# First product of three pairs of token groups by one level of Strassen

## The chip, the core and the metric

The kernel runs on one core of a Trainium2 chip. The core has a matrix engine (TensorE, in the profile PE, its weight loads PEld), a vector engine (VectorE, DVE), a scalar engine (ScalarE, ACT), GpSimd (POOL) and SyncE (SP), which here only issues DMAs; sixteen DMA engines move data between DRAM and the on-chip memory. Matmuls write to PSUM, which has eight banks of 128 x 512 float32. Every engine works through its own queue in order and waits on semaphores for the others. The metric is the device time of one execution in microseconds (us).

## What is computed

For each of 8 batches the reference makes a linear attention with 8 heads, 576 positions and 64 dimensions per head: softmax of k over the positions, softmax of q over the dimensions, `kv = k_s^T v`, and `x = q_s kv`. The 8 x 576 = 4608 rows of x, 512 wide, then go through a gated network:

```python
h = x @ w_in          # 512 -> 2048
g = h * np.cos(h)
out = g @ w_out       # 2048 -> 512
```

All of it is in float32. A float32 value is used by TensorE in two ways here: as one slower float32 matmul, or as the sum of a high and a low part in the rounded type float32r, with three matmuls (high x high, high x low, low x high).

## The kernel before

**Groups and units.** The 4608 tokens are nine groups of 512: 512 tokens of each batch (groups 0 to 7), and the 64 tokens left of each of the eight batches together (group 8, kept in DRAM in `x_left` until then). The 2048 columns of w_in are 16 blocks f of 128. A *unit* is one group with one f. `unit1` makes its first product, h = x w_in[f] (4 chunks of the 512 inputs x 3 matmuls = 12 matmuls into one PSUM bank, L866), and the gate: `turns` on ACT (L872), `rest` on DVE (L876), `cos` on ACT (L882), `gate` on DVE (L888), then the split into `ghi` on ACT (L892) and `glo` on DVE (L896). `unit2` makes the second product, g w_out[f], 4 x 3 matmuls (L935) that accumulate over f in four PSUM banks `acc`; it stands two units behind `unit1`. The first six units use float32 matmuls in the second product (L928). Groups 0 and 1 are interleaved by halves of the 16 f, with the half-finished output in DRAM (`part`); the others run over all f. `out_rows` takes the result from `acc` (ACT, L974, or with a part to be added DVE, L971) and writes it out.

**Weights.** The two weight matrices come as float64, are loaded raw (`load_w`), turned to float32 by two ACT and two DVE steps (`convert`) and split into high and low parts, which then stay on chip for all groups, w_in and w_out of each f beside each other (`w_io`) for f from 8 on.

**Attention.** `attend` for batch b is spread over the units of the group before it: `k_exps` (maximum over positions with GpSimd's all-reduce, L524, subtraction, exp), `k_steps` (kv, L571, and its normalisation), `q_steps` (softmax of q), `x_steps` (q transposed, from batch 2 on through DRAM in blocks; x product, `x_mm`, L730; x split by ACT `x_hi`, L744, and DVE `x_lo`, L758). For batches 0 and 1 (XF=2) `x_mm` is one float32 matmul; for the others it is three float32r ones, with kv and q split by L586, L606, L610 and L708, L718. Two PSUM banks, `att`, serve it; two, `h`, the first product.

**Order.** Nothing is issued in the order of the loops. Each step is put into a `Plan` with its engine, an estimated duration, the places that it reads and writes and, for some, a due time. `Plan.order` simulates all engines with these durations and latencies (the table `LAT`; ACT's table loads count only where `tables` is not zero, and it is 0) and picks each engine's next piece by priority among the ready ones; the order found is each engine's program order. Buffers are reused in rings (`BUFS`, `ring`).

All DMAs are issued by SP.

Of the kernel before, what the change touches and what calls it, by code (L numbers as in the profile page):

```python
# [27 lines left out]
    XF=2,  # L28
    PELO=1,
    early=1,  # L30
    F2=6,
# [12 lines left out]
    att1=(5.98, 6.97),  # L44
    att=dict(k=(0.32, 0.1), kv=(3.88, 1.0), q=(5.03, -0.91), qt=(22.82, 6.17), x=(4.44, 4.38)),
# [14 lines left out]
class Plan:  # L60
# [7 lines left out]
    LAT = {("ACT", "PE"): 0.37, ("DVE", "PE"): 0.3, ("DVE", "ACT"): 0.14, ("DVE", "DVE"): 0.13,  # L68
# [32 lines left out]

    def lat(self, i, j):

        a, b = self.steps[i], self.steps[j]
        return self.LAT.get((a[0], b[0]), 1.0 if a[0] == "BUS" else 0.2)

    def run(self, edges, prio, release=None, tables=False):
# [14 lines left out]
        for _ in range(n):  # L122
# [12 lines left out]
            while w and w[0][0] <= t:  # L135
                at, i = heappop(w)
                heappush(c, (at if e == "BUS" else prio[i], i))
# [57 lines left out]
def linear_attention_then_cos_gated_mlp(  # L195
# [54 lines left out]
    mask = const.tile([P, 2, 1], F32, name="mask")  # L250
    nc.vector.memset(mask, 0.0)
    nc.vector.memset(mask[0:D, 0], 1.0)
    nc.vector.memset(mask[D:P, 1], 1.0)
# [12 lines left out]
    def v_frame(t):  # L266
# [15 lines left out]
    part = dr.tile([2, NJ, P, DM], F32, name="part")  # L282

# [5 lines left out]
        x4k=8, kq=2, qm=1, qs=2, ql=1, mt=1, m1=1, m=2, r=2, kvt=1, kvw=4, xl=4, stage=2, wc=1, r2=3, ghi=2,  # L289
        glo=2, h=2, acc=4, att=2, qb=1, qf=1, qd=2,  # L290
# [13 lines left out]
    def sbt(shape, dt, tag, name, bufs=None):  # L304
        pool = small if tag in SMALL else sb
        return pool.tile(shape, dt, tag=tag, name=name, bufs=bufs or BUFS[tag])


    for tag, size in (
        ("pad", NL), ("ql", NL), ("qm", 18), ("qs", 18), ("r", 1),  # L310
        *((f"w{w}{f}", 2 * DM) for f in range(CFG["FN"]) for w in "io"),
        *((f"w{f}", 4 * DM) for f in range(CFG["FN"], NF)),
        ("x4k", 2 * TB), ("r2", TB), ("ghi", TB), ("glo", TB), ("stage", TB), ("wc", 2 * DM),
        ("kvw", 2 * P), ("mt", 4 * P), ("m1", 2 * P), ("m", 2 * P), ("kvt", P), ("xl", NL), ("kq", 4 * NC * D), ("qt0", S), ("qt1", S), ("qb", S), ("qf", S),
    ):
        for i in range(BUFS.get(tag, 1)):
            sbt([P, size], F32, tag, f"place_{tag}_{i}", BUFS.get(tag, 1))

    def bank(tag, name):
        return ps.tile([P, 512], F32, tag=tag, name=name, bufs=BUFS[tag])  # L320
# [10 lines left out]
    def room(f):  # L331


        return ("room", NF - 1 - f // 4, f % 4)

    def rooms(f):
        return [("room", f, i) for i in range(4)]

    def spot(ws, f):
        return f"w{f}" if f >= FN else f"w{ws}{f}"  # L340

    def load_w(w, f, after=0.0, seq=()):
        def load():
            if ("raw", w, f) not in T:
                ws = w if f < FN else "io"
                a = sbt([P, len(ws), DM, 2], U32, spot(ws, f), f"raw_{ws}{f}", 1)
                for i, x in enumerate(ws):
                    T["raw", x, f] = a, a[:, i]
# [12 lines left out]
            1.5, load, writes=[("w", w, f)] + rooms(f), after=after if not seq else 0.0, seq=seq  # L361
        )

    def convert(ws, f):

        n = len(ws)
        R = [("w", w, f) for w in ws]
        wait = ws == "o" and f < F2
        C = room(f) if wait else ring("wc")

        def low():
            return T["raw", ws[0], f][0][:, :, :, 0]

        def high():
            return T["raw", ws[0], f][0][:, :, :, 1]
# [17 lines left out]
        def sign():  # L393
            if wait:
                if ("room", f // 4) not in T:
                    T["room", f // 4] = sbt([P, 4, DM], F32, f"w{NF - 1 - f // 4}", f"room_{f // 4}", 1)
                c = T["wc", ws, f] = T["room", f // 4][:, f % 4 : f % 4 + 1]
            else:
                c = T["wc", ws, f] = sbt([P, 2, DM], F32, "wc", f"wc_{ws}{f}")[:, 0:n]
# [739 lines left out]
```

## Time and profile before

| | |
|---|---|
| Median of 3 runs | 889.59 us (889.19 to 890.18) |
| Span of the profiled execution | 885.9 us |
| Mean granted TensorE clock | 0.992 |
| Matmuls | 4336 |

The profile is of one execution; for it the page gives the span, from the first to the last instruction, and no time of its own. What lies around the span is taken from the median, 3.7 us. In the rows of groups, the columns are line, engine, operation, output and inputs with partitions and elements, the count, busy time in us and mean ns of one, and the idle time of the engine just before them with what ended it. In rows of the timeline they are start and length in us, engine, line, operation. In rows by stretch they are the stretch, its length, the busy time of PE, PEld, DVE, ACT and POOL with counts, the granted clock, the busy share of the DMA engines and GB/s. DMA rows give the size in KB and the us from issue to landing.

### The profile page before, as it was taken

Reading aid. Unit: us, or ns where it says so; the run is one execution under the profiler, and the core shown is the slowest. Engines: PE = TensorE matmul, PEld = TensorE weight load, DVE = VectorE, ACT = ScalarE, POOL = GpSimd, SP = SyncE. Lnnn points to the kernel's source line nnn. Section 1 sums busy time; section 2 is a strip of 40 time slices with the busy share of each in tenths; the row PEclk is TensorE's granted clock in tenths of the full one; section 3 lists DMA queues with packets and bytes.
Section 4 is the critical chain, followed back from the end, with each engine's and each line's share of the span. In section 5 each row is a group of like instructions: output and inputs, shape, how many; then the busy total and the mean of one; then the engine's idle time right before and its main releaser. Section 6 shows DMA issues by size and latency. Waiting matters only on the chain.

```text
span 885.9 us, 11763 instructions
## 1 busy us (share of the span) xinstructions
PE 866.2 (98%) x4336; PEld 705.2 (80%) x4336; DVE 555.0 (63%) x924; ACT 487.7 (55%) x812; POOL 30.3 (3%) x61
## 2 busy tenths in 40 slices
PE   6989999999999999999999999999999999999997
PEld 5656788887888888888888888888888888888885
DVE  7888888977686457745775568646853353333332
ACT  3898798566445545653675456635633353333332
POOL 1200100000000000100000000000000000000000
PEclk8999999999999999999999999999999999999999
DMA  8971656532363026302540046103410020001002
GB/s 228 293 214 35 203 182 185 142 106 76 84 177 82 1 57 180 84 2 57 134 117 15 22 122 140 41 4 105 109 25 1 3 96 1 1 0 48 1 1 48
DMA packets 167225, 75.75 MB, mean 86 GB/s; under 512 B 111360, under 2 KB 157952, under 8 KB 167168
## 3 DMA queue, kind: packets, MB, share of 16 engines
q1 hardware_dynamic: 167168, 75.00, 31.4%
q8 instruction: 34, 0.56, 0.3%
q14 instruction: 23, 0.19, 0.1%
HBM read 55.31 MB, written 19.66 MB: 85 GB/s over the span
## 4 chain that ended last, share of the span: by engine, by line
PE 90%; ACT 4%; DMA 2%; SPq 2%; DVE 1%; issue 1%; ACTq 0%
PE acc L935 42%; PE h L866 42%; PE x_False L730 3%; PE kv L571 2%; PE acc L928 1%; DMA k<-in_k_dram 1%; DMA raw_o<-in_moe_w_out_dram 1%; SPq L467 1%; ACT raw_o L378 0%; DMA v_sb<-in_v_dram 0%; SPq L463 0%; ACT w_i L409 0%; ACT L882 0%; ACT L646 0%; ACT raw_i L383 0%
## 5 line engine op out<-in xcount | busy, mean ns | idle before, releaser
L866 PE MATMUL h<-x,w_i 128*128 128x512 f32 x768 | 186.4, 391 | 0.5 <-DVE g L888 0.3
L866 PE MATMUL h<-x,w_io 128*128 128x512 f32 x768 | 185.4, 390 | 0.9 <-DVE kt L888 0.9
L935 PE MATMUL acc<-w_io,ghi 128*128 128x512 f32 x576 | 178.2, 390 | 0.1
L876 DVE SCALAR_TENSOR_TENSOR kt<-kt,h 128x512 f32<-128x512 int32 x144 | 98.4, 683 | 124.6 <-ACT kt L872 124.1
L872 ACT ACTIVATE kt<-h 128x512 int32<-128x512 f32 x144 | 86.0, 597 | 159.3 <-PE h L866 158.9
L866 PEld LDWEIGHTS h<-x,w_i 128*128 128x128 f32 x768 | 143.3, 188 | 31.2 <-ACT x L756 0.6
L866 PEld LDWEIGHTS h<-x,w_io 128*128 128x128 f32 x768 | 143.1, 188 | 30.9 <-DVE kt L888 1.5
L935 PE MATMUL acc<-w_o,ghi 128*128 128x512 f32 x528 | 163.8, 391 | 0.0
L888 DVE TENSOR_TENSOR kt<-kt,h 128x512 f32<-128x512 f32 x138 | 94.6, 685 | 76.1 <-ACT kt L882 75.2
L882 ACT ACTIVATE kt<-kt 128x512 f32<-128x512 f32 x144 | 91.1, 633 | 84.3 <-DVE kt L876 83.9
L892 ACT CAST ghi<-kt 128x512 fp32r<-128x512 f32 x138 | 85.5, 620 | 89.1 <-DVE kt L888 70.6
L896 DVE TENSOR_TENSOR glo<-kt,ghi 128x512 fp32r<-128x512 f32 x138 | 95.2, 690 | 62.7 <-ACT ghi L892 62.0
L935 PEld LDWEIGHTS acc<-w_io,ghi 128*128 128x128 f32 x576 | 107.2, 188 | 22.5 <-ACT o L974 0.8
L935 PEld LDWEIGHTS acc<-w_o,ghi 128*128 128x128 f32 x528 | 98.4, 188 | 20.5
L935 PE MATMUL acc<-w_io,glo 128*128 128x512 f32 x288 | 112.1, 389 | 0.0
L935 PE MATMUL acc<-w_o,glo 128*128 128x512 f32 x264 | 102.8, 389 | 0.0
L935 PEld LDWEIGHTS acc<-w_io,glo 128*128 128x128 f32 x288 | 54.1, 188 | 11.3
L935 PEld LDWEIGHTS acc<-w_o,glo 128*128 128x128 f32 x264 | 49.6, 188 | 10.4
L730 PE MATMUL x_False<-qt,kvw 128*128 128x288 f32 x176 | 34.9, 323 | 0.4 <-ACT qt L713 0.4
L744 ACT CAST x<-x_False 128x288 fp32r<-128x288 f32 x64 | 23.7, 370 | 18.2 <-PE x_False L730 18.2
L882 ACT ACT_TABLE_LOAD x26 | 33.4, 1283 | 0.4
L730 PEld LDWEIGHTS x_False<-qt,kvw 128*128 128x128 f32 x176 | 28.4, 191 | 5.5 <-POOL m L524 0.8
(103 smaller groups left out, 738.5 us busy)
## 6 DMA issues: line engine op xcount, KB each, us to landing
q<-in_q_dram SPq DMA_DIRECT2D x32, 256.0 KB, 3.4
out_dram<-o SPq DMA_DIRECT2D x32, 256.0 KB, 2.8
v_sb<-in_v_dram SPq DMA_DIRECT2D x30, 256.0 KB, 3.7
k<-in_k_dram SPq DMA_DIRECT2D x14, 512.0 KB, 4.6
qb<-q_rows SPq DMA_DIRECT2D x96, 72.0 KB, 2.5
q_rows<-q SPq DMA_DIRECT2D x24, 256.0 KB, 2.4
raw_i<-in_moe_w_in_dram SPq DMA_DIRECT2D x8, 512.0 KB, 5.5
raw_o<-in_moe_w_out_dram SPq DMA_DIRECT2D x8, 512.0 KB, 6.6
```

Source lines behind the costliest of these rows:

```text
L467: nc.sync.dma_start(t[NL * i : NL * (i + 1), 2 * CM, :].rearrange("p (h d) -> p h d", h=2), s2[:, NM:S, :].rearrange("h p d -> p h d"),)
L571: nc.tensor.matmul(x[h * D : (h + 1) * D, odd : odd + vt.shape[1]], t[:, h, c, :], vt, start=(c == CM), stop=(c == CM - 1),)
L730: nc.tensor.matmul(t[:, 0:HALF], a, c[:, cs], start=(n == 0), stop=(n == len(parts) - 1 and not again))
L744: nc.scalar.copy(T["x", b, p][:, 0, cs], o[:, 0 : cs.stop - cs.start])
L866: nc.tensor.matmul(o, a, x, start=(c == 0 and n == 0), stop=(c == KC - 1 and n == 2))
L872: nc.scalar.activation(t, T["h", u], AF.Identity, bias=0.25, scale=1.0 / TWO_PI)
L876: nc.vector.scalar_tensor_tensor(t.bitcast(F32), t, -TWO_PI, T["h", u], op0=ALU.mult, op1=ALU.add)
L882: nc.scalar.activation(t, t, AF.Sin, bias=0.5 * math.pi)
L888: nc.vector.tensor_mul(o, t, T["h", u])
L892: nc.scalar.copy(t, T["kt", u].bitcast(F32))
L896: nc.vector.tensor_sub(t, T["kt", u].bitcast(F32), T["gh", u].bitcast(F32))
L935: nc.tensor.matmul(T["acc", j], a[:, js], w, start=(first and n == 0), stop=(last and n == 2))
```

## The change

Groups 0 to 2 keep the form above (`std=3`). Groups 3 to 8 are worked in the pairs (3, 4), (5, 6), (7, 8). Within a pair, the first product of two groups and two blocks f, f+1 of w_in is made by one level of Strassen's scheme in Winograd's form: the 2 x 2 parts are the two groups by the two halves of the 512 inputs, and the two halves of the inputs by the two f. Seven products of sums of operands stand for eight, and further sums, made from the results in PSUM, give the four h.

- *Sums of w_in.* Each converted block of w_in is written to DRAM (`w_rows`, `keep`). During group 2 `sums(n)`, one for each of the 8 pairs of f, reads two of them, makes four sums on DVE, splits them and writes them, with the three operands that need no sum, to `w_sums` in DRAM. w_in itself then no longer stays on chip. In the pairs each `block` loads its seven operands (high and low parts) in four DMAs of up to 512 KB from POOL's queue, which converts float32 to float32r, into a ring of five buffers (`sr`, places of w_in 0 to 4).
- *Sums of x.* From batch 3 on x goes to DRAM whole (`x_main`, `x_row`). `x_sums` loads the two groups' halves and makes the seven operands on DVE and ACT, in places of w_in 8 to 15 and of x.
- *Products.* `block` issues seven products of 2 chunks x 3 matmuls, in turn into a bank of `h` and the second bank of `att`, which leaves one bank for the attention of later batches; three partial results are copied out by ACT and three added up by DVE, and the gates follow.
- *Second product.* Unchanged in form. `acc` has room for one group, so in each half of the 16 f (four blocks) the second products of one group (`now`) run among the blocks, and those of the other (`later`), whose g are kept in `stash`, after them. One group's output is parted by halves, as groups 0 and 1 were.
- *Attention.* `XF=8`: the x product is one float32 matmul for all batches, and the split of kv and q (`kv_norm`, `kv_hi`, `kv_lo`, `q_hi`, `q_lo`) is gone. Batches 3 and 4 are attended before the first pair, 5 and 6 beside it, 7 beside the second.
- *Places.* From f = 8 on, blocks of w_in, and of w_out, are converted in twos of the same matrix; buffers are named one by one.

The core of the diff:

```diff
-    XF=2,
+    XF=8,
...
+    std=3,
+    spans={2: (15.0, 28.0), 3: (24.0, 38.0), 4: (32.0, 47.0)},
...
+    def cast_load(self, us, fn, reads=(), writes=(), due=None):
+
+        t = object()
+        self.add("POOL", 1.1, fn, reads=reads, writes=[*writes, t], due=due)
+        self.add("SWB", us, None, reads=[*reads, t], writes=writes)
...
+        def keep():
+            for i, x in enumerate(fs):
+                nc.sync.dma_start(w_rows[x], T["wc", w, f][:, i])
...
+        if not keep:
+            for i in range(2):
+                plan.add("ACT", 0.4, lambda i=i: x_row(i), reads=[xo[i]], writes=[xs])
+            plan.load(0.9, put, reads=[xs], writes=[("x_main", p, b), ("x_left", p, b)], parts=2)
+            return []
...
+    def sums(n):
...
+        def adds():
+            t = T["sum", n].rearrange("p f (k d) -> p (f k) d", k=2)
+            a11, a12, a21, a22 = (t[:, i] for i in range(4))
+            nc.vector.tensor_add(a22, a21, a22)
+            nc.vector.tensor_sub(a21, a11, a21)
+            nc.vector.tensor_sub(a11, a22, a11)
+            nc.vector.tensor_sub(a12, a12, a11)
...
+    def x_sums(k, b1, b2):
...
+            for i, m, sub in (
+                (0, A0, None),
+                (1, A0, (A0, A1, A0)),
+                (2, A0, (A0, B1, A0)),
+                (3, B1, None),
+                (4, A1, (A1, B1, A1)),
+                (5, B0, None),
+                (6, B0, (B0, B0, A0)),
+            ):
+                if sub:
+                    plan.add(
+                        "DVE", 0.69, lambda sub=sub, move=move: move(*sub),
+                        reads=at(sub[1]) + at(sub[2]) + [st[0], st[1]], writes=at(sub[0]),
+                    )
+                xp = x_places(i, c)
+                plan.add("ACT", 0.62, lambda i=i, m=m, hi=hi: hi(i, m), reads=at(m) + [st[m[0]]], writes=xp)
+                plan.add("DVE", 0.69, lambda i=i, m=m, lo=lo: lo(i, m), reads=at(m) + [st[m[0]]], writes=xp)
...
+    def block(k, n, b1, b2, flip, due):
+
+        z, aux = ring("h"), ("att", 1)
+        c1, c5, c2 = (ring("c") for _ in range(3))
...
+        for m in range(4):
+            place = wide(ring("sr")[1])
...
+                nc.gpsimd.dma_start(t, w_sums[n, :, 2 * m : e])
+
+            plan.cast_load(
+                2.0 if m < 3 else 1.2, load, reads=[("sums", n, i) for i in range(3)],
+                writes=[place, (place, 0), (place, 1)],
+            )
+            ws.append(place)
...
+        def product(i, to, first):
+            if first:
+                T["z" + to, k, n] = bank(z if to == "z" else aux, f"{to}_{k}_{n}_{i}")
+            o = T["z" + to, k, n]
+            for c in range(2):
+                xh, xl = (T["xs", k, i, c][:, m] for m in range(2))
+                wh, wl = (T["s", k, n, i][:, m, c * P : (c + 1) * P] for m in range(2))
+                for m, (a, x) in enumerate(((wh, xh), (wh, xl), (wl, xh))):
+                    nc.tensor.matmul(
+                        o, a, x, start=(first and c == 0 and m == 0), stop=(c == 1 and m == 2),
+                        skip_group_check=not first,
+                    )
...
+        pe(0, "z", True)
+        copy("z", c1)
+        pe(1, "a", True)
+        copy("a", c5)
+        pe(2, "z")
+        copy("z", c2)
+        pe(3, "a")
+        add("a", c2)
+        G[b2, f] = post(0, b2, f, c2)
+        pe(4, "z")
+        add("z", c5)
+        G[b2, f + 1] = post(1, b2, f + 1, c5)
+        pe(5, "a", True)
+        add("a", c1)
+        G[b1, f] = post(2, b1, f, c1)
+        pe(6, "z")
+        G[b1, f + 1] = post(3, b1, f + 1, z)
+        return G
...
+    def pair(k, b1, b2, clk):
...
+        for half in range(2):
+            now, later = (b1, b2) if half == 0 else (b2, b1)
...
+            for n in range(NB * half, NB * half + NB):
+                G.update(block(k, n, b1, b2, half == 1, clk))
+                clk += 7 * 1.37 * phi
+                for e in range(2):
+                    if n > NB * half:
+                        f = 2 * (n - 1) + e
+                        second(now, n - 1, e, (now, f, f == 0, False, False, half == 0))
+                    split(now, n, e)
...
+            for n, e in fs:
+                f = 2 * n + e
+                if half == 0:
+                    what = (later, f, f == 0, False, False, False)
+                else:
+                    what = (later, f, f == NF // 2, f == NF - 1, True, False)
+                second(later, n, e, what)
...
+            if u == 2 * NF:
+                for n in range(NF // 2):
+                    sums(n)
+    for b in range(STD, min(STD + 2, B)):
+        attend(b, spans[b], ("att", "att", "att"))
+    clk = when(NU)
+    for pk, (b1, b2) in enumerate(PAIRS):
+        length = 29.3
+        at = (clk - T0) / U
+        for i, b in enumerate((b1 + 2, b2 + 2)):
+            if b < B:
+                attend(b, (at + 13 * i, at + 13 * i + 14), ("att", "att", "att"))
+        clk = pair(pk, b1, b2, clk)
```

More of the change, by code (lines that the diff above doesn't have):

```diff
@@ L288, in linear_attention_then_cos_gated_mlp @@
     BUFS = dict(
-        x4k=8, kq=2, qm=1, qs=2, ql=1, mt=1, m1=1, m=2, r=2, kvt=1, kvw=4, xl=4, stage=2, wc=1, r2=3, ghi=2,
-        glo=2, h=2, acc=4, att=2, qb=1, qf=1, qd=2,
+        x4k=8, kq=2, qm=1, qs=2, ql=1, mt=1, m1=1, m=2, r=2, kvw=4, xs=1, stage=2, wc=2, r2=3, ghi=2,
+        glo=2, h=2, acc=4, att=2, qb=1, qf=2, qd=2, sr=5, c=4,
     )
@@ L331, in room, with rooms, base, spot @@
     def room(f):
[L334 to L340, printed above, removed]
+        return ("room", NF - 2 - 2 * (f // 4), f % 4)
+    def rooms(w, f):
+        return [("room", f - f % 2, i) for i in range(4)] if w == "o" else []
+    def base(f):
+        return f if f < FN else f - f % 2
+    def spot(w, f):
+        return f"w{w}{base(f)}"
     def load_w(w, f, after=0.0, seq=()):
@@ L360, in load_w, with convert @@
         plan.load(
-            1.5, load, writes=[("w", w, f)] + rooms(f), after=after if not seq else 0.0, seq=seq
+            1.5, load, writes=[("w", w, f)] + rooms(w, f), after=after if not seq else 0.0, seq=seq
         )
[L364 to L368, printed above, removed]
+    def convert(w, f):
+        fs = [f] if f < FN else [base(f), base(f) + 1]
+        n = len(fs)
+        R = [("w", w, x) for x in fs]
+        wait = w == "o" and f < F2
         C = room(f) if wait else ring("wc")
         def low():
-            return T["raw", ws[0], f][0][:, :, :, 0]
+            return T["raw", w, f][0][:, :, :, 0]
         def high():
-            return T["raw", ws[0], f][0][:, :, :, 1]
+            return T["raw", w, f][0][:, :, :, 1]
         def bias():
@@ L428, in convert @@
             split()
+        if w == "i":
+            plan.load(0.73 * n, keep, reads=[C], writes=[("rows", x) for x in fs], parts=n)
     def load_k(b, p0, np_, tag, due, seq=()):
-        places = quarters(ring(tag)) if tag == "x4k" else [(r, i) for r in [ring(tag)] for i in (0, 1)]
+        slot = ring(tag)
+        places = quarters(slot) if tag == "x4k" else [(slot, i) for i in (0, 1)]
         def frame():
-            t = sbt([P, 2 * np_, NC, D], F32, tag, f"k_{b}_{p0}")
+            t = sbt([P, 2 * np_, NC, D], F32, slot, f"k_{b}_{p0}")
             for i in range(np_):
@@ L854, in unit1 @@
         b, f = order[u][:2]
[L855 removed]
+        h = ring("h")
         def g1(chunks):
             if 0 in chunks:
[L859 removed]
+                T["h", u] = bank(h, f"h_{u}")
             o = T["h", u]
@@ L916, in unit1, with split_g, hi, lo @@
+    def split_g(u, g):
+        gh, gl = ring("ghi"), ring("glo")
+        def hi():
+            t = T["gh", u] = sbt([P, TB], F32R, gh, f"ghi_{u}")
+            nc.scalar.copy(t, T["g", u])
+        def lo():
+            t = T["gl", u] = sbt([P, TB], F32R, gl, f"glo_{u}")
+            nc.vector.tensor_sub(t, T["g", u], T["gh", u].bitcast(F32))
+        plan.add("ACT", 0.62, hi, reads=g, writes=[gh])
+        plan.add("DVE", 0.69, lo, reads=[*g, gh], writes=[gl])
         return [gh, gl]
     acc = {}
-    def unit2(u, g, due):
-        b, f, first, last, more, cont = order[u]
+    def unit2(u, what, g, due):
+        b, f, first, last, more, cont = what
+        plain = isinstance(u, int) and u < F2
@@ L953, in unit2, with out_rows @@
             for j in range(NJ):
-                out_rows(u, j)
-    def out_rows(u, j):
-        b, f, first, last, more, cont = order[u]
-        tag = "kq" if u == len(order) - 1 and j >= 2 else "stage"
-        s = ring(tag)
+                out_rows(what, j)
+    def out_rows(what, j):
+        b, f, first, last, more, cont = what
+        name = f"{b}_{f}_{j}"
+        pb = b % 2
+        tag = "kq" if what == final and j >= 2 else "stage"
+        at = s = ring(tag)
         if tag == "kq":
```

501 lines of the change are left out of this document (299 added, 202 removed).

## The prediction

> **What bounds the kernel now.** I read the head of the page first, then stretches of the span, then what TensorE waited for, then a stretch of the timeline.
>
> ```profile
> span 885.9 us, 11763 instructions
> PE 866.2 (98%) x4336; PEld 705.2 (80%) x4336; DVE 555.0 (63%) x924; ACT 487.7 (55%) x812; POOL 30.3 (3%) x61
> PE 90%; ACT 4%; DMA 2%; SPq 2%; DVE 1%; issue 1%; ACTq 0%
> ```
>
> The span is 885.9 us and the median of the three timed runs 889.6 us, so I count 3.7 us around the span and work on the median's scale. The last line is the chain that ended last: 90% of it is TensorE. A busy PE can still be a slow PE, so the stretches come next (busy time, with the granted clock, DMA share and GB/s at the end of each row).
>
> ```profile
> 0.00:60.00 60.00, 48.12 (x308) 35.09 (x309) 48.32 (x113) 43.86 (x88) 9.97 (x25) 0.91 0.90 265
> 60.00:340.00 280.00, 278.52 (x1380) 222.69 (x1379) 214.33 (x339) 183.31 (x295) 10.43 (x19) 1.00 0.39 110
> 340.00:525.00 185.00, 185.00 (x969) 153.58 (x968) 118.73 (x199) 103.69 (x168) 6.52 (x12) 1.00 0.31 76
> 712.00:886.00 174.00, 167.54 (x740) 138.43 (x738) 65.33 (x95) 63.57 (x105) 0.00 (x0) 0.99 0.07 22
> ```
>
> From 60 us on TensorE has no gap and the full clock. 60 to 340 us is what is left of groups 0 to 2; 340 to 525 us is two later groups with the attention of two batches beside them. DVE is busy 77% and 64% of these stretches, ACT 65% and 56%. The waits of TensorE confirm it: ten rows in all, of which these are the first and the last (total, times, longest).
>
> ```profile
> PE kv L571 <- DMA v_sb<-in_v_dram: 2.9, 1, 2.9
> PE h L866 <- ACT x L756: 0.2, 1, 0.2
> ```
>
> So a matmul that goes away is time that goes away, and any new wait of TensorE is time added. The timeline shows what one matmul is worth.
>
> ```profile
> 602.52 2.88 PE L866 MATMUL h<-x,w_io 128*128 128x512 f32 x12
> 605.24 0.61 PE L935 MATMUL acc<-w_io,ghi 128*128 128x512 f32 x2
> 605.44 0.60 ACT L872 ACTIVATE kt<-h 128x512 int32<-128x512 f32 x1 [2.27 <-PE h L866]
> ```
>
> Twelve matmuls of a first product take 605.24 - 602.52 = 2.72 us from start to start, 0.227 us each. (The 390 ns of the page's groups is latency; neighbours overlap.) The last result is there at 602.52 + 2.88 = 605.40, 0.16 us after the next work has begun, and ACT starts on it 0.04 us later.
>
> **The matmuls removed.** For a pair of groups and two columns f of w_in the kernel now issues 2 x 2 x 12 = 48 matmuls in the first product; block() issues 7 products of 6, that is 42. There are 3 pairs x 8 blocks = 24 blocks: 24 x 6 = 144 matmuls fewer, x 0.227 = **-32.6 us**. The second product (L935) keeps its count.
>
> **The attention's product.** XF=8 makes x_mm one float32 matmul for all batches, in place of three float32r ones for batches 2 to 7.
>
> ```profile
> 84.68 0.65 PE L730 MATMUL x_False<-qt,kvw 128*128 128x288 f32 x2
> 85.16 0.60 PE L683 MATMUL qt<-ident,q 128*128 128x128 f32 x4
> ...
> 565.83 0.96 PE L730 MATMUL x_False<-qt,kvw 128*128 128x288 f32 x6
> 566.63 2.92 PE L866 MATMUL h<-x,w_io 128*128 128x512 f32 x12
> ```
>
> The first two rows are batch 1: one float32 call holds TensorE 0.48 us. The last two are a later batch: two calls of three take 0.80 us. 6 batches x 4 x (0.96 - 0.80) = **+3.8 us**. With these two terms alone: 889.6 - 32.6 + 3.8 = 860.8 us. This is the floor; what follows is what TensorE may wait for.
>
> **The hand-over inside a block.** Products alternate between the bank z and the bank aux, and each needs its bank emptied (ACT copy) or added up (DVE add) while only one other product, 6 x 0.227 = 1.36 us, runs.
>
> ```profile
> L974 ACT COPY o<-acc 128x512 f32<-128x512 f32 x36 | 20.5, 585 | 6.6 <-DMA out_dram<-o 3.2 <-PE acc L935 2.7
> L971 DVE TENSOR_TENSOR o<-o,acc 128x512 f32<-128x512 f32 x8 | 5.4, 676 | 0.3 <-DMA o<-part 0.3
> ```
>
> ```profile
> 77.17 0.68 DVE L888 TENSOR_TENSOR g<-kt,h 128x512 f32<-128x512 f32 x1
> 77.90 0.50 PE L866 MATMUL h<-x,w_i 128*128 128x512 f32 x1 [0.27 <-DVE g L888]
> ```
>
> DVE's end at 77.85 released TensorE at 77.90. So the chain is 0.16 + 0.04 + 0.585 (or 0.676) + 0.05 = 0.84 (0.93) us: it fits in 1.36 us with 0.5 (0.4) us over, if the engine is free. If it must first finish another 0.68 us piece, TensorE is some 0.2 us late at the worst. Five hand-overs a block, 120 in all: 0 to 120 x 0.25 = 30 us. The second products (2.72 us each, 16 for every 28 products) can stand between, so I take the end near zero: **+3 us**.
>
> How full the engines are: per pair 24 copies (14 us) and 14 splits of operand sums (9 us) come to ACT, 24 adds (16 us), 20 steps of operand sums (14 us) and 4 output adds (3 us) to DVE. Splits go by these rows, and DVE loses the work of the second fence.
>
> ```profile
> L892 ACT CAST ghi<-kt 128x512 fp32r<-128x512 f32 x138 | 85.5, 620 | 89.1 <-DVE kt L888 70.6
> L896 DVE TENSOR_TENSOR glo<-kt,ghi 128x512 fp32r<-128x512 f32 x138 | 95.2, 690 | 62.7 <-ACT ghi L892 62.0
> ```
>
> ```profile
> L718 DVE TENSOR_TENSOR qt<-qf,qt 128x576 fp32r<-128x576 f32 x24 | 18.0, 749 | 1.1 <-ACT qt L708 1.1
> L586 DVE SCALAR_TENSOR_TENSOR kvt<-kv,r,mask 128x128 f32<-128x128 f32 x24 | 8.3, 344 | 0.3
> L610 DVE TENSOR_TENSOR kvw<-kvt,kvw 128x128 fp32r<-128x128 f32 x24 | 6.7, 280 | 2.2 <-ACT kvw L606 2.2
> L758 DVE TENSOR_TENSOR x<-x_False,x 128x288 fp32r<-128x288 f32 (+1 forms) x56 | 23.3, 416 | 9.0 <-ACT x L744 7.6 <-ACT xl L747 1.4
> ```
>
> Two batches shed 8 x (0.749 + 0.344 + 0.280 + 2 x 0.416) = 17.6 us. From the stretch 340 to 525 us: DVE 118.7 - 17.6 + 33 = 134 us, in a stretch of 185 - 48 x 0.227 + 1 = 175 us: 77% in place of 64%. ACT 104 + 23 = 127 us, 72% in place of 56%. Fuller, not full.
>
> **The table loads.** ACT loads a table whenever exp follows sin or the reverse.
>
> ```profile
> L882 ACT ACT_TABLE_LOAD x26 | 33.4, 1283 | 0.4
> L646 ACT ACT_TABLE_LOAD x14 | 18.0, 1283 | 0.3
> L537 ACT ACT_TABLE_LOAD x11 | 14.1, 1283 | 0.2
> ```
>
> 51 loads in 8 batches are 6.4 a batch. The order of the work comes from a model in the kernel that counts them as nothing (tables=0). Today the result of a first product is needed two units later, which hides a swap of 2 x 1.28 us; in a block the cover is 0.5 us. Batches 5 to 7 have their attention beside blocks: 19 loads x 1.28 = 25 us of ACT. Between 0 and 25 us; half of TensorE's time there is second products, and a delay once taken covers the next ones: **+4 us**.
>
> **The way into the first pair.** Operands of batch 4 go through DRAM: write, read back, split, multiply.
>
> ```profile
> part<-o SPq DMA_DIRECT2D x8, 256.0 KB, 2.4
> o<-part SPq DMA_DIRECT2D x8, 256.0 KB, 3.1
> raw_i<-in_moe_w_in_dram SPq DMA_DIRECT2D x8, 512.0 KB, 5.5
> raw_io<-in_moe_w_out_dram SPq DMA_DIRECT2D x8, 512.0 KB, 6.9
> ```
>
> 2.4 + 3.1 + 0.62 + 0.69 = 6.8 us after the last x of batch 4, or 9.2 us if the read, 512 KB in two parts, takes the 5.5 us of the third row. The second products of the last two units cover 5.4 us. If that x is early the cost is nothing; if it comes with the last first product, 1.4 to 3.8 us; if DVE, fuller than now, pushes it two units of 5.4 us back, 12 to 15 us. I take **+4 us**. Later pairs have ten second products, 27 us, behind their last block, which covers the same chain and the 13.8 us of DVE for the sums: 0.
>
> **The streams and the stages before.** Sums of w_in: 96 loads on POOL's queue, four a block, ring of 5 buffers. A buffer is refilled seven products (9.5 us) before its next use, or more with second products between; loads of 512 KB land in 5.5 to 6.9 us. No row shows a load issued by POOL or one that converts; bounds 0 and the 6.9 us row, cover holds: 0. Their volume, 24 x 1.8 MB, is some 80 GB/s on a path that moved 265 in the first 60 us. Making the sums costs DVE 8 x (4 adds + 1 split) by these rows:
>
> ```profile
> L518 DVE TENSOR_TENSOR m<-m,k 128x256 f32<-128x256 f32 (+1 forms) x18 | 6.9, 385 | 0.4
> L413 DVE TENSOR_TENSOR w_io<-wc_io,w_io 128x1024 fp32r<-128x1024 f32 x8 | 9.7, 1217 | 0.0
> ```
>
> 8 x (4 x 0.385 + 1.217) = 22 us; batch 4's attention, moved ahead of 340 us, adds about the 22 us that is left of a batch (118.7 - 32 x 2.06 for the gates, halved, is 26, less the lighter parts), while batches 2 and 3 shed 14 us. 214 + 30 = 244 of 280 us, 87%: **+2 us**, bounds 0 and 8. In the first 60 us the DMA engines are 90% busy and the first five or so writes of converted w_in (256 KB, 1 us each at 265 GB/s) join: **+1 us**, bounds 0 and 5.
>
> Sum: 860.8 + 3 + 4 + 4 + 2 + 1 = 874.8; the two ACT terms cover each other in part, so I say **873 us**.
>
> [...] The granted clock was 0.91 in the first 60 us and 1.00 after, and TensorE never idled over 2.9 us in between. [...]
>
> **Rivals.**
> *1. Hand-overs and table loads are paid in full share.* Against it: 0.4 to 0.5 us of room and second products between. For it: ACT 72%, DVE 77%, in-order queues. Half the upper bounds, 15 + 12, in place of 7: 893; a third: 886. Time 881 to 893, 0.17.
>
> *2. Slower: POOL's queue holds the stream back.* Loads stand in order behind the all-reduces and k frames of batches 5 to 7, and such a frame waits for its buffer:
>
> ```profile
> POOL k L440 <- DMA q_rows<-q: 194.9, 6, 57.4
> ```
>
> 6 such waits, up to 57.4 us. Batches 5 to 7 have 3 x 6 such POOL steps. The gain of 28.8 us is gone when each holds a load up 28.8 / 18 = 1.6 us past its cover; at 2.5 us it is 861 + 45 = 906. Against it: the order puts a step where its input is expected. [...] 0.13.
>
> *3. The clock drops at the pairs' entries.* The first 60 us lost 0.09 x 60 = 5.4 us to the clock. Three entries like that: 873 + 16 = 889. 0.05.
>
> *4. Every cover holds.* 860 to 865: 0.07. That the count of products isn't cut I exclude: the loops are written out.
>
> **Numbers.** Forecast 865 to 881: 0.58. A measurement of this kernel tells about 0.2% from no change, 887.8 to 891.4. Faster: 0.58 + 0.07 + 0.09 of rival 1 + 0.02 of rival 3 = 0.76. Same: 0.06 + 0.02 = 0.08. Slower: 0.13 + 0.02 + 0.01 = 0.16. The range 860 to 896 leaves out rival 2 and little else.
>
> **What would show it.** Matmuls on 128x512: 144 fewer. PE without gaps inside blocks, or waits of 0.2 us on copies and adds (hand-over), of 1 to 2.5 us beside exp (tables). One gap of about 4 us at the first block, on DMA or the split of x. Waits of TensorE on w_sums loads would be rival 2; a granted clock under 1.00 past 60 us rival 3. DVE about 77% and ACT 72% in the first pair. Wrong above all if TensorE's waits in the blocks exceed 29 us.

## The result, and the profile after

The kernel takes **926.53 us** after the change (four runs, 923.85 to 930.53) against 889.62 before: a ratio of 1.0416, with an interval of 1.0384 to 1.0448. It became about 37 us slower, where the prediction had said 873 us. The profiled run is the fastest of the four, 923.85 us, of which its span is 921.8.

The first lines of the page after, with the chain that ended last:

```profile
span 921.8 us, 12171 instructions
...
PE 859.0 (93%) x4144; PEld 677.9 (74%) x4144; DVE 617.6 (67%) x995; ACT 546.0 (59%) x910; POOL 88.6 (10%) x181
...
PE 48%; DMA 9%; ACT 6%; DVE 5%; issue 4%; SPq 3%; POOL 0%; ACTq 0%; DVEq 0%; POOLq 0%
```

There are 192 matmuls fewer: 144 of the first product, and 48 of the attention's (176 into x_False before at L730, 128 after at L712: a float32 one stands there as two, three fp32r ones as three). Yet TensorE is busy only 7 us less than before, and it was 98% of the span and is now 93%. Its share of the chain fell from 90% to 48%: the end is now set by TensorE and its suppliers in turn.

Stretches of the span, after; the columns are those of the prediction's table:

```profile
0.00:60.00 60.00, 45.19 (x290) 33.36 (x290) 45.16 (x104) 39.99 (x82) 9.39 (x25) 0.86 0.97 278
60.00:200.00 140.00, 137.68 (x667) 104.25 (x666) 123.99 (x189) 117.08 (x188) 10.17 (x18) 1.00 0.72 213
200.00:350.00 150.00, 135.91 (x671) 105.42 (x670) 109.68 (x176) 83.63 (x130) 8.12 (x21) 1.00 0.77 213
350.00:550.00 200.00, 183.41 (x909) 144.98 (x908) 129.49 (x204) 123.60 (x202) 27.13 (x53) 0.99 0.66 169
550.00:700.00 150.00, 141.40 (x672) 113.56 (x671) 92.00 (x145) 78.86 (x136) 16.39 (x31) 0.99 0.58 151
700.00:922.00 222.00, 215.44 (x944) 176.33 (x942) 117.29 (x180) 102.82 (x176) 17.43 (x33) 1.00 0.38 112
```

And two of these stretches before:

```profile
200.00:350.00 150.00, 149.12 (x804) 123.15 (x803) 100.19 (x173) 79.42 (x133) 5.09 (x9) 1.00 0.35 90
350.00:550.00 200.00, 200.00 (x1038) 166.11 (x1037) 131.27 (x218) 112.90 (x182) 8.17 (x14) 1.00 0.32 79
```

TensorE is idle for 14.1, 16.6 and 8.6 us between 200 and 700 us; before, it was idle 0.9 us in the first of these and not at all in the second. From 700 us on, where no attention stands beside the blocks, it is full but for the tail. So blocks run dense where nothing else stands beside them; the idle time is where attention, sums of w_in and blocks meet. The granted clock is 0.99 to 1.00 past 60 us.

What TensorE waited for, after (us in total, times, longest):

```profile
PE x_False L712 <- ACT xs L742: 24.4, 20, 2.9
PE kv L599 <- ACT k L561: 5.6, 2, 3.2
PE a L1152 <- ACT c L1166: 4.0, 2, 3.1
PE h L839 <- DVE kt L879: 3.3, 4, 1.6
...
PE a L1152 <- DMA s<-w_sums: 0.5, 1, 0.5
...
PE z L1152 <- DMA s<-w_sums: 0.3, 1, 0.3
```

The first row stands out. It is the attention's x product (L712) waiting for `x_row` (L742), ACT's copy of an x out of its bank: 20 waits, one for each of the four quarters of the five batches 3 to 7. The stream of w_in's sums, the prediction's way to "slower", is awaited for 0.8 us.

One of the 20 waits, in full. First, rows of the timeline of all engines:

```profile
406.00 1.35 DVE L646 TENSOR_REDUCE qm<-q 128x18 f32<-128x1152 f32 x1 [2.54 <-DMA q<-in_q_dram]
...
406.65 0.65 PE L712 MATMUL x_False<-qf,kvw 128*128 128x288 f32 x2
...
407.27 0.68 DVE L868 SCALAR_TENSOR_TENSOR stash<-stash,c 128x512 f32<-128x512 int32 x1
```

ACT's own timeline from there:

```profile
407.98 0.63 ACT L874 ACTIVATE stash<-stash 128x512 f32<-128x512 f32 x1 [3.86 <-DVE stash L868]
408.52 0.60 ACT L895 CAST ghi_('s', 0, 1, 2)_3840<-kt_('s', 0, 1, 2)_3681 128x512 fp32r<-128x512 f32 x1
409.15 1.28 ACT L653 ACT_TABLE_LOAD   x1
410.44 1.16 ACT L653 ACTIVATE q<-q 128x1152 f32<-128x1152 f32 x1
411.51 0.61 ACT L864 ACTIVATE kt_('s', 0, 2, 2)_3858<-c 128x512 int32<-128x512 f32 x1
412.03 0.60 ACT L895 CAST ghi_('s', 0, 1, 3)_3864<-kt_('s', 0, 1, 3)_3770 128x512 fp32r<-128x512 f32 x1
412.54 0.39 ACT L742 COPY xs<-x_False 128x288 f32<-128x288 f32 x1
```

And TensorE's:

```profile
409.67 0.39 PE L923 MATMUL acc<-w_o,glo_('s', 0, 0, 3)_3714 128*128 128x512 f32 x1
412.98 0.75 PE L712 MATMUL x_False<-qf,kvw 128*128 128x288 f32 x2 [2.92 <-ACT xs L742]
```

The first half of an x leaves TensorE at 406.65 + 0.65 = 407.30. Its copy takes 0.39 us but starts at 412.54, because six instructions stand ahead of it in ACT's queue, one a table load. And that queue had started late: it stood for 3.86 us behind a gate, whose step on DVE stood behind a reduction that waited for a q from DRAM. TensorE has work to 410.06; then its own queue is blocked by the second half of the x, which needs the one bank that the attention has left (its kv product and its transposes of q use the same bank). Before the change the two halves took the two banks of `att` in turn.

How all waits add up can't be read from that view alone, since a late matmul often shows as a spacing of 0.4 us and not as a wait. So I took each distance from start to start in the trace, less the usual one for its line, and summed what was over 0.1 us: 26 us before and 95 us after. From the first matmul to the last it is 877 us before and 915 after; without the late starts, 850.45 and 820.77. After, the 95 us stand ahead of the x product (37.9; 6.6 before), the blocks' products (15.0), the second product (14.9; 3.1), the first product of single groups (10.6; 3.9), kv (9.8; 7.0) and smaller ones. Of the 37.9 us at the x product, 24.4 are the waits for L742 shown above; the rest has other causes or shows as no wait.

### The profile page after: what moved, and what is told of

Its sections match the earlier page's. It is cut to its first block, busy times and chain, and to the rows that moved or that the text cites. A ratio compares the mean times of both kernels' runs of the same rounds, so it can differ in the third digit from the quotient of the medians.

```text
span 921.8 us, 12171 instructions
## 1 busy us (share of the span) xinstructions
PE 859.0 (93%) x4144; PEld 677.9 (74%) x4144; DVE 617.6 (67%) x995; ACT 546.0 (59%) x910; POOL 88.6 (10%) x181
## 3 DMA queue, kind: packets, MB, share of 16 engines
q0 software_dynamic: 13824, 44.05, 17.6%
## 4 chain that ended last, share of the span: by engine, by line
PE 48%; DMA 9%; ACT 6%; DVE 5%; issue 4%; SPq 3%; POOL 0%; ACTq 0%; DVEq 0%; POOLq 0%
PE acc L923 25%; PE z L1152 10%; PE a L1152 7%; PE h L839 4%; DMA q<-in_q_dram 3%; PE x_False L712 2%; DMA s<-w_sums 1%; DMA out_dram<-o 1%; SPq L490 1%; SPq L486 1%; PE kv L599 1%; ACT xs L742 1%; DMA w_sums<-sl 1%; DVE xs L1079 1%; DVE qm L646 1%
## 5 line engine op out<-in xcount | busy, mean ns | idle before, releaser
L1152 PE MATMUL z<-xs,s 128*128 128x512 f32 x576 | 148.3, 395 | 3.0 <-DVE kt L879 1.0
L1152 PEld LDWEIGHTS z<-xs,s 128*128 128x128 f32 x576 | 108.1, 189 | 27.9 <-DVE c L1173 2.5
L1152 PE MATMUL a<-xs,s 128*128 128x512 f32 x432 | 113.2, 398 | 4.6 <-ACT c L1166 4.0
L923 PE MATMUL acc<-w_o,ghi 128*128 128x512 f32 x336 | 108.1, 403 | 1.7 <-DVE o L961 1.1
L1152 PEld LDWEIGHTS a<-xs,s 128*128 128x128 f32 x432 | 81.5, 190 | 23.5 <-ACT c L1166 5.0
L1127 POOL DMA_DIRECT2D s<-w_sums x96 | 50.9, 531 | 415.4 <-PE a L1152 271.2
L712 PE MATMUL x_False<-qf,kvw 128*128 128x288 f32 x128 | 45.6, 444 | 28.7 <-ACT xs L742 24.4
L712 PEld LDWEIGHTS x_False<-qf,kvw 128*128 128x128 f32 x128 | 22.7, 197 | 43.3 <-ACT xs L742 32.9
L864 ACT ACTIVATE kt<-h 128x512 int32<-128x512 f32 x48 | 28.5, 594 | 29.0 <-PE h L839 26.5
L868 DVE SCALAR_TENSOR_TENSOR kt<-kt,h 128x512 f32<-128x512 int32 x48 | 32.6, 681 | 11.3 <-ACT kt L864 11.3
L874 ACT ACTIVATE kt<-kt 128x512 f32<-128x512 f32 x48 | 30.3, 633 | 15.9 <-DVE kt L868 15.5
L646 DVE TENSOR_REDUCE qm<-q 128x18 f32<-128x1152 f32 x16 | 21.6, 1350 | 24.4 <-DMA q<-in_q_dram 24.4
L879 DVE TENSOR_TENSOR kt<-kt,h 128x512 f32<-128x512 f32 x42 | 28.6, 680 | 13.6 <-ACT kt L874 13.4
```

Of the source, the lines that this page charges most:

```text
L646: nc.vector.tensor_reduce(out=m, in_=rows(), axis=AX.X, op=ALU.max)
L712: nc.tensor.matmul(t[:, 0:HALF], T["kv", b, p], T["qf", b, p][:, cs], start=True, stop=not again)
L864: nc.scalar.activation(t.bitcast(I32), src(), AF.Identity, bias=0.25, scale=1.0 / TWO_PI)
L868: nc.vector.scalar_tensor_tensor(t, t.bitcast(I32), -TWO_PI, src(), op0=ALU.mult, op1=ALU.add)
L874: nc.scalar.activation(t, t, AF.Sin, bias=0.5 * math.pi)
L879: nc.vector.tensor_mul(o, t, src())
```

## The experiments

Theory 1: the bank taken from the attention is the main loss. Its rivals: transfers that land later under the new DMA traffic, that of the sums and that of the stream (theory 2 in the expectations), the table loads (theory 3), the blocks' own hand-overs. Four edits leave every engine's order of work as it was, but for what they add or leave out, as the traces show: the first three below and the doubled stream. All others let the kernel's model lay out a new order, which can change the time by itself; no run here says by how much. The kernel before, run beside them, had medians from 889.3 to 889.7 us. Behind each median stand the ratio to it and its interval; "less" without more is against the changed kernel's 926.53.

**Two banks for batches 3 and 4**, which are attended when no block runs yet:

```diff
-            t = T["xp", b, p, i, again] = bank(ob[i] if again else xo[i], f"x{i}_{b}_{p}_{again}")
+            t = T["xp", b, p, i, again] = bank(
+                ("att", 1) if b in (3, 4) and i else ob[i] if again else xo[i], f"x{i}_{b}_{p}_{again}"
+            )
```

> Same program order as the changed kernel; the second x product of batches 3 and 4 goes into the second bank of att, which no block uses yet. Theory 1 (the single PSUM bank: the second x product waits until ACT has emptied the first): the waits of TensorE before L712 between 200 and 350 us, some 11 us together, nearly vanish, and the time falls by 8 to 11 us to 916 to 919. Theory 2 (DMA traffic delays loads, and the engines' queues behind them) or theory 3 (ACT table loads): TensorE waits elsewhere instead, 923 to 928.

Measured: 918.71 us, 1.0311 (1.0282 to 1.034); 8 us less. As theory 1 had it:

```profile
PE x_False L714 <- ACT xs L744: 14.7, 12, 2.4
```

Twelve waits are left, those of batches 5 to 7; 8 waits and 9.7 us are gone. TensorE's idle time from 200 to 350 us fell from 14.1 to 7.2 us:

```profile
200.00:350.00 150.00, 142.79 (x729) 112.92 (x726) 115.50 (x188) 89.06 (x141) 9.62 (x22) 1.00 0.78 214
```

This is the cleanest test of theory 1: the order of work is the same, and only the place of these products differs.

**No second half of x:**

```diff
         def x_mm(i, again=False):
+            if i and not keep:
+                T["xp", b, p, i, again] = T["xp", b, p, 0, again]
+                return
```

> Leaves out the second half of the x product for batches 3 to 7 (the first half is copied twice); the rest stands in the same order. The 20 calls left out take 20 x 0.48 = 9.6 us. Theory 1: their waits go as well, 25 to 31 us, so 886 to 893. Theories 2 and 3: ACT and DVE are as late as before, TensorE waits for the next copy or add, and only the 9.6 us and a little are gained: 912 to 918.

Measured: 896.29 us, 1.0072 (1.0046 to 1.0098). Of the 30.2 us, 20 matmuls of 0.48 us are 9.6; the other 20.6 us are time that TensorE waited (15 us by the count of late starts, which compares the slowest run of this kernel with the fastest of the changed one). That is most of theory 1's amount and not all: with the x waits gone, the blocks' products were late by 21.8 us in place of 15.0.

**No table swaps:**

```diff
-            nc.scalar.activation(t, t, AF.Exp)
+            nc.scalar.activation(t, t, AF.Exp if b < 3 else AF.Identity)
```

> Leaves out exp for batches 3 to 7 (Identity stands in its place), so ACT loads no tables for them; same order. Theory 3: some 32 loads of 1.28 us go, and with them 15 to 25 us: 902 to 912. Theory 1: ACT is less late, so the waits for the bank shrink a little: 918 to 925. Theory 2: 924 to 927.

Measured: 916.92 us, 1.0301 (1.0268 to 1.0334); 9.6 us less, between the two. The trace has 38 table loads fewer. They are a part of the loss, and in part by way of the same bank, for the x waits fell too:

```profile
PE x_False L712 <- ACT xs L742: 18.7, 20, 2.1
```

**One pair only**: groups 0 to 6 go singly as before the change, groups 7 and 8 as a pair, the sums are made in group 6, and spans and due times are set to match.

```diff
-    std=3,
+    std=7,
...
-            if u == 2 * NF:
+            if u == 6 * NF:
```

> One part alone: only groups 7 and 8 as a pair (std=7), with no attention beside the blocks; the other groups in the old form, the float32 x product kept. Floor 889.6 - 48 x 0.227 + 3.8 = 882.5. Theory 1: only batch 7 has one bank, some 5 us: 884 to 890. If the blocks themselves or the stream cost what was lost, a third of the 66 us over the floor is paid here: 900 to 906.

Measured: 906.79 us, 1.0188 (1.0173 to 1.0203): far over theory 1's range, and 0.8 us over that of its rival. Yet the bank is at work here too, with a longer wait than I had priced. The waits row, then ACT's timeline ahead of the longest, then TensorE's:

```profile
PE x_False L712 <- ACT xs L742: 11.2, 4, 6.3
```

```profile
629.04 1.28 ACT L653 ACT_TABLE_LOAD   x1
630.33 1.16 ACT L653 ACTIVATE q<-q 128x1152 f32<-128x1152 f32 x1
...
632.39 1.04 ACT L1005 CAST sh<-sum 128x1024 fp32r<-128x1024 f32 x1
...
633.94 1.28 ACT L874 ACT_TABLE_LOAD   x1
...
636.23 0.40 ACT L742 COPY xs<-x_False 128x288 f32<-128x288 f32 x1
```

```profile
628.34 0.65 PE L712 MATMUL x_False<-qf,kvw 128*128 128x288 f32 x2
...
636.69 1.33 PE L712 MATMUL x_False<-qf,kvw 128*128 128x288 f32 x2 [6.31 <-ACT xs L742]
637.40 4.81 PE L839 MATMUL h<-x,w_i 128*128 128x512 f32 x12
642.05 0.62 PE L923 MATMUL acc<-w_o,ghi 128*128 128x512 f32 x2
```

Even in a stage of single groups, one bank costs 6.31 us where two table loads, an exp and a split of the sums stand ahead of the copy.

**One pair, two banks.** Beside that pair no attention runs, so the second bank is simply there:

```diff
-        xo = [spare(tx, b), spare(tx, b)]
+        xo = [spare(tx, b), spare(tx, b)] if keep else [("att", 0), ("att", 1)]
```

> One pair (groups 7 and 8) as before, with two banks for the x product of batch 7. Theory 1: the four waits of 11.2 us go, 894 to 898. Theory 2 (the engines are late because the sums of w_in and their DMAs stand in that group): 900 to 906, with waits before other instructions between 600 and 700 us.

Measured: 891.53 us (10 runs), 1.0023 (1.0012 to 1.0033): 15.3 us less than with one bank, and under theory 1's range. The stretch from 600 to 700 us, first with one bank and then with two:

```profile
600.00:700.00 100.00, 88.36 (x398) 70.21 (x397) 66.55 (x105) 49.84 (x83) 1.10 (x3) 0.95 0.65 190
```

```profile
600.00:700.00 100.00, 98.10 (x462) 80.02 (x461) 73.68 (x118) 55.64 (x93) 1.10 (x3) 1.00 0.65 195
```

TensorE is 9.7 us busier there, at the full clock; by the count of late starts, 19.1 us became 3.9. One line was edited, and the gain lies in the stretch where it acts. The order of work is the same up to 608 us, within this batch, and differs from there on, so a part of the 15.3 us may be the order's; the waits that went are 11.2 us.

**Two banks with all three pairs** (`beside`). For this x must not stand inside a block, which uses both banks; so `attend` became a generator that hands one quarter of a batch to the order before each block. `xo` is as in the last diff, and the model that finds the order gets two rounds more.

```diff
-    rounds=8,
+    rounds=10,
...
         for p in range(NP):
+            yield
             xr += x_steps(
...
             for n in range(NB * half, NB * half + NB):
+                next(side, None)
                 G.update(block(k, n, b1, b2, half == 1, clk))
```

> Gives the x product of batches 3 to 7 two banks in a full kernel: the second half goes to the bank of the blocks' aux, and the attention of batches 5 to 7 is handed to the plan one quarter between two blocks, so that aux is free there (rounds=10 in place of 8, which alters the order a little). Theory 1 (one bank): the 31 us of added waits before L712 mostly go, 896 to 904. If ACT and DVE are late by themselves (theories 2 and 3), TensorE waits for the copies and adds of the blocks or for aux: 912 to 925.

Measured: 908.94 us, 1.0218 (1.0188 to 1.0249): 17.6 us less, between the two. No wait for L742 is left at the x product, and one of 1.8 us has come at a product of a block, which now shares its bank. 82 us of late starts are left: 15.0 at the x product in place of 37.9, but 20.4 and 17.4 at the second product and the first product of single groups, in place of 14.9 and 10.6. 19 us of all stand from 200 to 350 us.

**The same, with table loads counted in the model** (and the rounds as they were):

```diff
-    rounds=10,
+    rounds=8,
-    tables=0,
+    tables=0.01,
```

> As beside, and the plan counts each table load with 1.28 us (tables=0.01; rounds=8). Theory 3 as a part of the loss: 5 to 10 us under beside. If table loads matter only through the single bank: as beside within 3 us.

Measured: 902.97 us, 1.0142 (1.012 to 1.0164): 6 us less than `beside`. The two orders differ almost from the start, so this is what one order gains on another, and not a price of the loads alone.

**The stream twice.** Each load of w_sums is issued twice, into the same buffer:

```diff
                 nc.gpsimd.dma_start(t, w_sums[n, :, 2 * m : e])
+                nc.gpsimd.dma_start(t, w_sums[n, :, 2 * m : e])
```

> The changed kernel with every load of w_sums issued twice: 88 MB in place of 44 MB from POOL's queue, all else in the same order. Theory 2 in the form that the stream slows the loads of the attention: 932 to 945. Theories 1 and 3: 924 to 930.

Measured: 1083.57 us, 1.2179 (1.2145 to 1.2213): far off every expectation. What TensorE and what POOL waited for:

```profile
PE z L1153 <- DMA s<-w_sums: 94.8, 18, 11.1
```

```profile
POOL s L1128 <- DMA s<-w_sums: 426.7, 94, 8.9
```

The second load isn't issued until the first has landed, a wait of 4.5 us on average, while a load lands as before (4.3 us in the median, 4.4 in the changed kernel). So this prices loads that follow each other in POOL's queue, and not a doubled volume. By an estimate from these rows, the four loads of a block hold that queue for 4 x (0.53 + 4.5 + 0.53) = 22 us; in the changed kernel three blocks' worth of products (the first 126) took 415.0 - 357.3 = 57.7 us, 19 us a block, and here 451.3 - 361.9 = 89.4 us. In the changed kernel a load takes 0.53 us of POOL and lands in 4.4, within the 9.5 us of seven products, and TensorE waited 0.8 us for the stream: there it is hidden.

**The sums' traffic on POOL's queue** in place of SP's, on top of `beside_tables` (reads and writes of `w_rows`, writes to `w_sums`):

```diff
-                nc.sync.dma_start(w_rows[x], T["wc", w, f][:, i])
+                nc.gpsimd.dma_start(w_rows[x], T["wc", w, f][:, i])
```

> As beside_tables (902.97), with the DMAs that make the sums of w_in (w_rows, its reading, w_sums) issued from POOL's queue in place of SP's. If the remaining waits before 350 us come from SP's queue, behind which the loads of q, k and v stand: they fall by 6 to 10 us, 893 to 897. If they come from the traffic on the DMA engines or from the work of the sums on DVE and ACT: 900 to 906.

Measured: 909.01 us, 1.0207 (1.0188 to 1.0226): 6 us more than `beside_tables`, and over both ranges. So SP's queue isn't what makes these transfers dear, or what it costs is less than what POOL's queue and the new order cost.

**Sums copied, not made**, on top of `beside`:

```diff
-        plan.add("DVE", 1.5, adds, writes=[s])
-        plan.add("ACT", 1.1, hi, reads=[s], writes=quarters(hs))
-        plan.add("DVE", 1.22, lo, reads=[s, *quarters(hs)], writes=quarters(ls))
```

> As beside (908.94); leaves out the sums of w_in (four more operands are copied to w_sums by DMA in their place), so DVE loses 22 us and ACT 9 us of work in group 2 while about the same bytes are written. If that work on full queues is what delays TensorE in group 2: 897 to 902. If the DMA traffic does: 905 to 911.

Measured: 904.2 us (897.99 to 908.2), 1.0155 (1.0111 to 1.0199): 4.7 us less than `beside`, with runs that overlap those of `beside`. Late starts from 200 to 350 us fell from 19 to 9.6 us and grew elsewhere. It decides nothing.

**Two pairs, from group 5 on**, as `beside_tables`, with the sums in group 4 and spans and due times set to match:

```diff
-    std=3,
+    std=5,
...
-            if u == 2 * NF:
+            if u == 4 * NF:
```

> Two pairs (groups 5 to 8), two banks for the x product as in beside, table loads counted, sums of w_in made in group 4. Floor 889.6 - 96 x 0.227 + 3.8 = 871.6. Theory 1 with the losses seen so far (front 5, one group with sums and attention 4, batch 7 beside a pair 5 to 8): 885 to 889. If the loss grows with anything else in the blocks: 892 to 900.

Measured: 899.85 us, 1.0114 (1.0099 to 1.0129): a miss for theory 1 with the losses seen so far, and within the range that I gave for a loss that grows with something else. Its stretch from 450 to 600 us holds 23 of its 64 us of late starts, with the DMA engines 80% busy:

```profile
450.00:600.00 150.00, 135.54 (x631) 106.75 (x630) 108.75 (x173) 88.39 (x147) 12.72 (x26) 0.98 0.80 211
```

**No trip of w_in through DRAM.** The sums need w_in as float32; the changed kernel writes it to `w_rows` early on and reads it back. Here DVE adds the two parts that lie on chip:

```diff
-            nc.sync.dma_start(t, w_rows[f : f + 2].rearrange("f p d -> p f d"))
+            for i in range(2):
+                w = T["w", "i", f + i].bitcast(F32)
+                nc.vector.tensor_add(t[:, i], w[:, 0], w[:, 1])
...
-        if w == "i":
-            plan.load(0.73 * n, keep, reads=[C], writes=[("rows", x) for x in fs], parts=n)
```

First with one pair and two banks, then with all three (`beside_tables`):

> As one_pair_two_banks (891.53), without w_rows: the sums of w_in take its high and low parts on chip (DVE adds them, 11 us more in all). If the writes to w_rows in the first 60 us delay the start (DMA engines 94% busy there): 885 to 888, under the kernel before. If the start is late for another reason: 890 to 893.

> As beside_tables (902.97), without w_rows, three pairs. If these DMAs are what is late in the first 60 us and in group 2: 893 to 898. If the work of the sums on DVE is, which grows by 11 us: 903 to 908.

Measured: 889.29 us (11 runs), 1.0003 (0.9994 to 1.0012) with one pair, 2.2 us less than with the trip; 902.81 us, 1.015 (1.0131 to 1.0169) with three, no less. With 11 us of DVE's work put in its place, leaving out the trip gains nothing for three pairs.

**The two versions that might beat both kernels**: one pair on chip with table loads counted, and two pairs on chip (attention handed out between the blocks as in `beside`, table loads not counted).

> As one_pair_on_chip, with each table load counted in the plan. Where TensorE has no short hand-over beside exp, table loads are hidden: within 1.5 us of one_pair_on_chip. If they cost by themselves: 2 us or more under it.

> Two pairs with two banks for x, without w_rows, table loads not counted. Floor 871.6. With the start as before and some 12 us in group 4 and beside the first pair: 882 to 887, under the kernel before. If the sums and two attentions in one group cost as before: 893 to 899.

Measured: 888.41 us (median of 11 runs), 0.9979 (0.9967 to 0.999), and **887.76 us** (12 runs), 0.9986 (0.9977 to 0.9996). Both are faster than the kernel before by 1 to 2 us, about what can be told from no change. Counting the table loads gained 0.9 us by the medians and 2.1 us by the ratios, which decides nothing between its two expectations. In the second, the stretch from 450 to 600 us:

```profile
450.00:600.00 150.00, 145.02 (x684) 117.15 (x683) 117.24 (x188) 94.31 (x156) 15.21 (x29) 0.98 0.75 200
```

TensorE is 9.5 us busier there than in the two pairs with the trip, and the whole is 12 us shorter. Two edits stand between these kernels (the trip, the counting of tables), so the 12 us can't be put down to the trip alone.

## Why the prediction was wrong, step by step

| Step | predicted | shown |
|---|---|---|
| products removed, x product as one float32 matmul | -28.8 | -29.7 (850.45 to 820.77 us without late starts) |
| hand-over inside a block | +3, bounds 0 and 30 | +15.0 late at L1152 |
| table loads | +4, bounds 0 and 25 | 9.6 less without them |
| way into the first pair | +4, bounds 0 and 15 | 0.99 of wait, on a gate (row below) |
| DVE in the stages before | +2, bounds 0 and 8 | 14.1 idle from 200 to 350 us (0.9 before; 7.2 with two banks for batches 3 and 4) |
| first 60 us | +1, bounds 0 and 5 | TensorE 2.9 less busy, clock 0.86 for 0.91 |
| stream of the sums of w_in | 0 | 0.8 of waits |
| one bank for the attention's x | not there | 24.4 of waits for L742; +31.3 late at L712 in all |
| second product and first product of single groups | not there | +11.8 and +6.7 late |

The rows overlap and are not a sum. In the count of late starts the sum is -29.7 + 68.3 = +38.6 us, by which the first matmul and the last stand further apart than before.

The way into the pair, in TensorE's timeline, is the wait ahead of the first product of the first block:

```profile
357.30 1.67 PE L1152 MATMUL z<-xs,s 128*128 128x512 f32 x6 [0.99 <-DVE kt L879]
```

**The count was right.** The matmuls that went away are worth about what two timeline rows said, 0.227 us each: 29.7 us in place of 28.8.

**The step that failed** is "The hand-over inside a block". It said that products "alternate between the bank z and the bank aux", and asked what this costs the products. It did not ask whose bank aux had been. It was the attention's second one, and the sum has no term for its loss. From batch 3 on the two halves of an x share one bank, and the second waits for a copy that takes 0.39 us but goes through ACT's queue in order, behind whatever stands there. The waits for this copy are the largest single part, 24.4 us; late starts at the x product grew by 31.3 us in all. The runs bear the cause out: 8 us back for two of five batches with the order of work unchanged, 20.6 us beyond the work itself without the second half, 15.3 us from the one line in the kernel with one pair. With two banks and all pairs 17.6 us came back and not 31; other waits took part of the place. So the bank is shown for some 18 to 24 of the 66 us over the floor; it is the main single cause, and less than half of the loss.

**Table loads and hand-overs** were the right mechanisms with sizes too small; both lie inside their bounds. That the bounds hold is in part luck, for I priced the loads beside the blocks only. The trace shows them ahead of the x copy as well, so the two terms feed one another and can't be added up: without the loads, the x waits fell by 5.7 us (24.4 to 18.7).

**The stages before** failed in kind. The forecast of DVE's work was near (244 us of 280, 87%; the rows from 60 to 350 us give 124 + 110 = 234 of 290, 81%), as was that in the first pair (134 us of DVE and 127 of ACT; 129.5 and 123.6 shown from 350 to 550 us, in a stretch of 200 us where 175 were forecast, so 65% and 62% busy). From "fuller, not full" I took that little is awaited. But from 200 to 350 us DVE and ACT are 73% and 56% busy, and TensorE stands still for 14 us. About half of that is the bank (8 of the 20 waits; 7.2 us are left when they go). Transfers that land later stand in the chain as well; how much they add, no run here separates. Three pieces of the chain from 270 to 300 us (start, us, what), and the loads of q, before and after (last number: median us to landing):

```profile
277.01 2.54 SPq L490
...
282.48 7.11 DMA w_sums<-sl
...
293.89 3.57 DMA q<-in_q_dram
```

```profile
q<-in_q_dram SPq DMA_DIRECT2D x32, 256.0 KB, 3.4
```

```profile
q<-in_q_dram SPq DMA_DIRECT2D x32, 256.0 KB, 5.4
```

One issue of a q stands 2.54 us in SP's queue, a write of the sums lands after 7.11, and the loads of q take 5.4 us in place of 3.4. The DMA engines are 77% busy from 200 to 350 us, and were 35%.

**The rivals.** Rival 2, the stream, isn't it: 0.8 us; with the loads doubled, TensorE did wait for it, once POOL's queue was held for longer than a block lasts. The loads of 512 KB landed in 4.4 us (median), and the trace shows no hold-up that TensorE felt beyond these 0.8 us. Rival 3, the clock, is a small part: 0.99 of 350 us, some 3 us. Rival 1 had the mechanism of late copies, but beside the blocks only, and without the bank. None of them foresaw 95 us of late starts. Rival 1's time, 881 to 893 us, lies 33 us and more under the one measured; rival 2's 906 us lay nearer, by another mechanism.

**What stays open** is how the 42 us that the best version with three pairs still has over the floor (902.8 against 860.8) divide among the making of the sums, the traffic, the order, and the blocks' hand-overs. POOL's queue made it worse, leaving out the sums' arithmetic gave 4.7 us with overlapping runs, leaving out the trip gave none. As each of these edits gives a new order, differences of this size can't be pinned to one cause.

## What to carry to other kernels

When a change takes a buffer or a bank, price what the former owner now has to do in turn: find the instruction that empties the one that is left, and count what stands ahead of it in its engine's queue, not how long it takes itself. This kernel, at 98% of TensorE, could gain from fewer matmuls only as far as its order held other ready work at each new hand-over; busy shares of some 70% on the helpers did not show whether it did. A room of half a microsecond in an order made by a model is small beside what the model left out here: table loads of 1.28 us, and loads that land 2 us later.

## What was not expected of the hardware

*The clock after a wait.* In the kernel with one pair, the 12 matmuls after the wait of 6.31 us take 642.05 - 637.40 = 4.65 us from start to start, in place of 2.72. In the changed kernel the same happens after a shorter one:

```profile
383.58 2.66 PE L1152 MATMUL a<-xs,s 128*128 128x512 f32 x6 [3.10 <-ACT c L1166]
386.17 1.32 PE L599 MATMUL kv<-v_sb,k 128*64 128x66 f32 x20
```

Six matmuls take 2.59 us in place of 1.36 after 3.10 us. After the 2.92 us at 412.98 there was no such loss, while at 605.60, after waits of 2.63 and 0.96 us, twelve matmuls took 4.44 us in place of 2.72. The granted clock tells these apart. In the trace of the changed kernel it goes to half at 383.91 and at 605.78 us, each time for 3.4 us, and stays at 1.00 around the wait at 412.98. The 3.41 us ahead of each fall and the 3.41 us at half clock behind it, and between them the two such stretches that meet at 412.98:

```profile
380.50:383.91 3.41, 0.33 (x1) 0.30 (x2) 3.41 (x5) 3.40 (x6) 0.53 (x1) 1.00 0.74 232
383.91:387.32 3.41, 3.41 (x26) 2.46 (x24) 3.34 (x7) 0.60 (x2) 0.53 (x1) 0.50 0.03 11
409.57:412.98 3.41, 0.49 (x4) 0.07 (x2) 2.80 (x5) 3.38 (x6) 0.00 (x0) 1.00 1.02 156
412.98:416.39 3.41, 3.41 (x15) 2.79 (x16) 3.05 (x7) 2.75 (x4) 0.20 (x1) 1.00 0.16 53
602.37:605.78 3.41, 0.90 (x3) 0.48 (x4) 2.79 (x5) 0.20 (x1) 0.00 (x0) 1.00 1.11 345
605.78:609.19 3.41, 3.41 (x9) 2.63 (x10) 3.41 (x5) 2.17 (x4) 0.50 (x1) 0.50 0.52 61
```

The length of one wait does not decide, for the clock fell after waits of 2.63 and 0.96 us and not after one of 2.92. Nor does TensorE's busy time just ahead, for it fell after 0.90 us and not after 0.49. What does decide, no run here shows. With one pair, the granted clock was 0.71 from 630 to 640 us and 0.95 from 640 to 650. In the cases shown the half clock cost 1.2 us (2.59 - 1.36), 1.7 us (4.44 - 2.72) and, with one pair, 1.9 us (4.65 - 2.72).

*A second load into the same buffer* was held back until the first had landed: 94 waits of POOL, 426.7 us. POOL's queue waits there on a semaphore of the first load, so these runs show how the program orders two writes of one buffer, and no limit of the chip.
